# Two of the 32 output stores of a linear-attention kernel, cut by partitions into six transfers each

## The chip, the cores and the metric

The kernel runs on one core of a Trainium2 chip. A core has five engines with instruction streams of their own: TensorE (PE in the profile), VectorE (DVE), ScalarE (ACT), GpSimd (POOL) and SyncE (SP). It also has 16 DMA engines, which move data between the chip's main memory (HBM) and the on-chip memory (SBUF, 128 partitions). Here SP issues every transfer but one. The metric is the device time of one execution in microseconds (us); smaller is better. The time before is 171.07 us, the median of three runs (171.04 to 171.13).

## The reference

The inputs `q`, `k`, `v` are bf16, of one batch, 32 heads, 2048 rows and 128 columns. Every head is computed by itself:

```python
phi_q = where(q > 0, q + 1, exp(q)) + 1e-6
phi_k = where(k > 0, k + 1, exp(k)) + 1e-6
kv  = einsum("bhsd,bhse->bhde", phi_k, v)
z   = einsum("bhsd->bhd", phi_k)
num = einsum("bhqd,bhde->bhqe", phi_q, kv)
den = einsum("bhqd,bhd->bhq", phi_q, z)[..., None] + 1e-6
out = num / den
```

An input or an output of one head is 2048 x 128 bf16 values, 512 KB. The kernel reads three such blocks for each head and writes one: 50.33 MB in, 16.78 MB out.

## The kernel before

One head is one step of the pipeline. Its 2048 rows are laid out so that partition `p` holds the 16 rows `16p` to `16p + 15` (`rows`, L228): in SBUF and in HBM alike a partition's share is one contiguous run of 4096 bytes. A transfer of one head is therefore 128 runs of 4096 bytes (for `v`, 256 runs of 2048 bytes, because the tile in SBUF has a gap in the middle).

For each head (`for h in range(NH)`, L264) the kernel loads k, v and q (L281), forms the two parts of phi_k on ACT, POOL and DVE (L289 to L300), multiplies them with v on PE (L316, L319), transposes q on PE (L335), forms phi_q on ACT and DVE (L346 to L355), multiplies it with kv on PE (L370, L371), and divides by the denominator on DVE (L391, L397, L415, L419). In the last three heads a part of the division runs on ACT (L406, table `TAIL`). The result of a head lies in one of ten output buffers, `o_sb[:, bo]` with `bo = h % 10`, and goes to HBM by the store of L431.

The order of every engine's stream is written out by hand. `Plan.add` takes an engine, a key, what the operation reads and writes, and for a transfer the semaphore that it raises. `Plan.order` (L54) sorts each engine's operations by key, and `Plan.emit` (L60) puts the necessary waits ahead of each. A wait stops all that stands behind it in the same stream. At its end SP waits until the semaphore of every store has its full count (L118 to L121).

On SP, the loads of head `h` have keys `h - 7.95` (k), `h - 6.9` (q) and `h - 6.8` (v), and the store of head `h` has the key of this line:

```python
            late = h + 1.0 + 0.18 * h
```

So the stores fall further and further behind their heads. The last loads, those of head 31, have keys up to 24.2. The store of head 20 has the key 24.6, so the stores of heads 20 to 31 are all issued after the last load, in order of heads: ten whole ones, then head 30 in two pieces and head 31 in three (table `PIECES`, L181). Heads 22 and 25 are among the whole ones. Their buffers, 2 and 5, are not written again by any later head.

Of the kernel before, what the change touches and what calls it, by code (L numbers as in the profile page):

```python
# [144 lines left out]
def bass_standalone__linear_attn_elu__prompt_kernel(  # L145
# [8 lines left out]
    NT = 16  # L154
# [3 lines left out]
    NBI = 6  # L158
    NBO = 10
# [20 lines left out]

    PIECES = {NH - 2: ((0, 6), (6, NT)), NH - 1: ((0, 6), (6, 12), (12, NT))}  # L181
    EXTRA = {NH - 2: 0, NH - 1: 1}

    qf = q.rearrange("b h s d -> (b h) s d")
    kf = k.rearrange("b h s d -> (b h) s d")
    vf = v.rearrange("b h s d -> (b h) s d")
    of = out.rearrange("b h s d -> (b h) s d")

    with ExitStack() as es:
        def sb(name, shape, dt):  # L190
            return es.enter_context(nc.sbuf_tensor(name, shape, dt))
# [14 lines left out]
        o_sb = sb("o_sb", [P, NBO, NT, D], bf16)  # L206
# [11 lines left out]
        def dma_sem(name):  # L218
            return dsems[name]

        for n, c in (("k", NBI), ("q", NBI), ("v", NBI), ("o", NBO + 3), ("x", 2)):
            for i in range(c):
                dsems[(n, i)] = es.enter_context(nc.semaphore(f"s_{n}{i}"))

        block = es.enter_context(nc.Block())
        pl = Plan()

        def rows(x, h):  # L228
            return x[h].rearrange("(p j) d -> p (j d)", j=NT)
# [7 lines left out]
               reads=[("id0",)], writes=[("ident",)])  # L237
# [26 lines left out]
        for h in range(NH):  # L264
# [3 lines left out]
            bi, b2, b3, bo = h % NBI, h % 2, h % 3, h % NBO  # L268

            def load(name, buf, src, key, h=h, bi=bi):  # L270
# [7 lines left out]
                if name == "v":  # L278
# [11 lines left out]
                   reads=[("k", bi)], writes=[("ek", b2)])  # L290
            pl.add("pool", h, lambda g, bi=bi, b3=b3: g.tensor_scalar(rk_sb[:, b3, :], k_sb[:, bi, :], BIG, 0.0,  # L291
                                                                      op0=ALU.min, op1=ALU.max),
                   reads=[("k", bi)] + ([("emq", 1)] if h == 2 else []), writes=[("rk", b3), ("rkx", b3), ("phik", b3)])
            pl.add("dve", at("emk", -3 + 0.95),
                   lambda d, b2=b2, b3=b3: d.tensor_scalar(emk_sb[:, b3, :], ek_sb[:, b2, :], 1.0, EPS, op0=ALU.min, op1=ALU.add),  # L295
                   reads=[("ek", b2)], writes=[("emk", b3)])

            def added(x, b3=b3):
# [3 lines left out]
                reads=[("emk", b3), ("rkx", b3)] + ([("emq", (h - 1) % 3)] if h else []), writes=[("phik", b3)])  # L302

            def kv(pe, tiles, srcs, h=h, bi=bi, b3=b3):
                for j in tiles:
# [17 lines left out]
                   reads=[("emk", b3), ("rk", b3), ("v", bi), ("ones",), ("vones",)], writes=[("bankkv",)])  # L323
            pl.add("pe", at("kv", -1.2), lambda pe, kv=kv: kv(pe, ADD, (rk_sb,)), reads=[("phik", b3), ("v", bi)], writes=[("bankkv",)])
            pl.add("act", at("kvs", -0.95), lambda a, b3=b3: a.activation(kvs_sb[:, b3, 1:], kvz_ps[:, 1:NC], ACT.Copy),
                   reads=[("bankkv",)], writes=[("kvs", b3)])
            pl.add("dve", at("zs", -1 + 0.905), lambda d, b3=b3: d.tensor_scalar(  # L327
                kvs_sb[:, b3, 0:1], kvz_ps[:, 0:1], kvz_ps[:, NC:NC + 1], None, op0=ALU.add),
                   reads=[("bankkv",)], writes=[("zs", b3)])
# [14 lines left out]
            for half in (0, 1):  # L344
                pl.add("act", h - 1.1 + 0.05 * half,
                       lambda a, b2=b2, c=cols(half): a.activation(eq_sb[:, b2, c], xT_ps[:, c], ACT.Exp),  # L346
                       reads=[("bankx", half)], writes=[("eq", b2, half)])
            pl.add("act", h - 1.0,
                   lambda a, b3=b3, c=cols(1): a.activation(rq_sb[:, b3, c], xT_ps[:, c], ACT.Relu),  # L349
                   reads=[("bankx", 1)], writes=[("rq", b3, 1)])  # L350
            pl.add("dve", at("rq", -2 + 0.948),
                   lambda d, b3=b3, c=cols(0): d.tensor_scalar(rq_sb[:, b3, c], xT_ps[:, c], 0.0, None, op0=ALU.max),  # L352
                   reads=[("bankx", 0)], writes=[("rq", b3, 0)])
            pl.add("dve", at("emq", -2 + 0.955),
                   lambda d, b2=b2, b3=b3: d.tensor_scalar(emq_sb[:, b3, :], eq_sb[:, b2, :], 1.0, EPS, op0=ALU.min, op1=ALU.add),  # L355
                   reads=[("eq", b2, 0), ("eq", b2, 1)], writes=[("emq", b3)])
# [4 lines left out]
            def nbank(b, h=h):  # L361
                return ("bankx", b) if h == NH - 1 and b < 2 else ("banko", b)
# [48 lines left out]
            for g, (b0, b1, place_d, runs) in enumerate(groups):  # L411
# [6 lines left out]
                    reads=banks, writes=[("den", b3, g)])  # L418
                pl.add("dve", key + 0.01, lambda d, b3=b3, b0=b0, b1=b1: d.reciprocal(  # L419
                    rden_sb[:, b3, 4 * b0:4 * b1], den_sb[:, b3, 4 * b0:4 * b1]),  # L420
                    reads=[("den", b3, g)], writes=[("rden", b3, g)])
                if g == 0:
                    pl.add("dve", h + 0.911, last_tile, reads=[nbank(0), nbank(1), ("rden", b3, 0)], writes=[("o", bo, NT - 1)])
                for n, (eng, t0, t1, *place_a) in enumerate(runs):
                    pl.add(eng, h + place_a[0] if eng == "act" else key + 0.012 + 0.004 * n,
                           div_act(t0, t1) if eng == "act" else div(t0, t1),
                           reads=[nbank(b) for b in range(t0 // 3, (t1 + 2) // 3)] + [("rden", b3, g)],
                           writes=[("o", bo, t) for t in range(t0, t1)])

            def store(t0, t1, key, slot, h=h, bo=bo):  # L430
                pl.add("sp", key, lambda sp: sp.dma_start(rows(of, h)[:, t0 * D:t1 * D],  # L431
                                                          o_sb[:, bo, t0:t1].rearrange("p j d -> p (j d)")),
                       reads=[("o", bo, t) for t in range(t0, t1)], dma=("o", slot))

            late = h + 1.0 + 0.18 * h
            for n, (t0, t1) in enumerate(PIECES.get(h, ((0, NT),))):
                store(t0, t1, late + 0.01 * n, bo if n == 0 else NBO + EXTRA[h] + n - 1)

# [29 lines left out]
```

## Time and profile before

| What | Value |
|---|---|
| Median of three runs | 171.07 us |
| The profiled execution's own time | 171.07 us |
| Its span, from the first to the last instruction | 169.3 us |
| Granted TensorE clock, mean | 0.967 |
| Busy: PE, ACT, DVE, POOL | 159.0, 157.3, 149.7, 106.1 us |
| Moved by DMA | 67.56 MB, mean 399 GB/s |
| Stores issued by SP | 35: 30 of 512 KB, five smaller |

The time of the execution is 1.8 us longer than its span; that part lies outside what the profile shows. A busy share is the part of the span in which an engine had an instruction in work. The DMA share is the mean over the core's 16 DMA engines; because neighbouring packets of one engine overlap a little in the record, an engine that never pauses shows slightly more than 1.

### The profile page before, as it was taken

The page shows a single profiled execution, that of the slowest core. Times are in us where ns is not written, and L with a number is a line of the kernel's source. Part 1 is how long each engine was busy: PE and PEld are TensorE (multiplying, and loading weights), DVE is VectorE, ACT ScalarE, POOL GpSimd, SP SyncE. Part 2 cuts the span into 40 slices and gives each one's busy share as a digit, 9 for nine tenths or more (in the row PEclk, how much of TensorE's full clock was granted, in tenths as well). Part 3 has the DMA queues.
Part 4 walks back from the last instruction along what each step waited for, and adds up shares of the span by engine and source line. Part 5 has one row for each costly group of instructions (what it writes and reads, how often), then busy time and mean ns, then how long its engine had stood idle before and what let it go on. Part 6 is the DMA issues. An engine that isn't in the chain of part 4 may idle for free.

```text
span 169.3 us, 7126 instructions
## 1 busy us (share of the span) xinstructions
PE 159.0 (94%) x3116; PEld 158.0 (93%) x3116; DVE 149.7 (88%) x293; ACT 157.3 (93%) x179; POOL 106.1 (63%) x72
## 2 busy tenths in 40 slices
PE   7499999999999999999999999999999999999940
PEld 7399999999999999999999999999999999999830
DVE  0253899999999999999999999999999999999870
ACT  3789999999999999999999999999999999996960
POOL 2586866666677766666677766666667776666000
PEclk9957999999999999999999999999999999999995
DMA  5999999999999999999999999999999999999985
GB/s 190 415 416 408 416 408 406 406 406 415 409 411 409 413 413 411 414 412 411 418 410 411 417 407 412 413 414 411 413 413 411 411 415 413 409 416 415 401 348 195
DMA packets 22862, 67.56 MB, mean 399 GB/s; under 512 B 2096, under 2 KB 2608, under 8 KB 22832
## 3 DMA queue, kind: packets, MB, share of 16 engines
q1 hardware_dynamic: 22688, 66.59, 98.6%
q8 instruction: 24, 0.39, 0.9%
q10 hardware_dynamic: 144, 0.52, 0.8%
q14 instruction: 6, 0.05, 0.1%
HBM read 50.33 MB, written 16.78 MB: 396 GB/s over the span
## 4 chain that ended last, share of the span: by engine, by line
PE 90%; DMA 3%; DVE 3%; ACT 1%; issue 0%
PE kvz_ps L316 38%; PE o_ps L370 17%; PE x_ps L335 17%; PE o_ps L371 17%; DMA k_sb<-in_k_dram 3%; DVE o_sb L397 1%; PE kvz_ps L319 1%; ACT ek_sb L289 1%; DVE emk_sb L295 0%; DVE rden_sb L419 0%; DVE den_sb L415 0%; DVE o_sb L391 0%; DVE kvs_sb L327 0%
## 5 line engine op out<-in xcount | busy, mean ns | idle before, releaser
L300 POOL TENSOR_TENSOR rk_sb<-rk_sb,emk_sb 128x640 bf16<-128x640 bf16 x32 | 44.8, 1399 | 45.1 <-DVE emq_sb L355 41.3
L289 ACT ACTIVATE ek_sb<-k_sb 128x2048 bf16<-128x2048 bf16 x32 | 69.4, 2169 | 3.0 <-DMA k_sb<-in_k_dram 3.0
L346 ACT ACTIVATE eq_sb<-x_ps 128x1024 bf16<-128x1024 bf16 x64 | 69.5, 1258 | 2.2 <-PE x_ps L335 2.2
L316 PE MATMUL kvz_ps<-v_sb,rk_sb 128*128 128x128 bf16 (+1 forms) x512 | 69.0, 220 | 0.0
L397 DVE TENSOR_TENSOR o_sb<-o_ps,rden_sb 128x768 bf16<-128x768 f32 (+2 forms) x63 | 68.0, 1119 | 0.1
L291 POOL TENSOR_SCALAR rk_sb<-k_sb 128x2048 bf16<-128x2048 bf16 x32 | 61.1, 1909 | 5.0 <-DMA k_sb<-in_k_dram 3.4
L370 PE MATMUL o_ps<-kvs_sb,emq_sb 128*128 128x129 bf16 (+1 forms) x536 | 61.1, 217 | 0.3 <-DVE o_sb L397 0.3
L371 PE MATMUL o_ps<-kvs_sb,rq_sb 128*128 128x129 bf16 (+1 forms) x536 | 61.1, 217 | 0.0
L316 PE MATMUL kvz_ps<-v_sb,emk_sb 128*128 128x128 bf16 (+1 forms) x352 | 56.5, 221 | 1.5 <-DVE emk_sb L295 1.5
L319 PE MATMUL kvz_ps<-ones_sb,rk_sb 128*128 128x1 bf16 x388 | 53.9, 167 | 0.0
L370 PEld LDWEIGHTS o_ps<-kvs_sb,emq_sb 128*128 128x128 bf16 x536 | 50.6, 98 | 0.5 <-DVE o_sb L397 0.4
L371 PEld LDWEIGHTS o_ps<-kvs_sb,rq_sb 128*128 128x128 bf16 x536 | 50.1, 97 | 0.0
L316 PEld LDWEIGHTS kvz_ps<-v_sb,rk_sb 128*128 128x128 bf16 x512 | 47.8, 99 | 0.0
L349 ACT ACTIVATE rq_sb<-x_ps 128x1024 bf16<-128x1024 bf16 x32 | 40.6, 1270 | 0.0
L319 PE MATMUL kvz_ps<-ones_sb,emk_sb 128*128 128x1 bf16 x228 | 38.1, 168 | 0.0
L316 PEld LDWEIGHTS kvz_ps<-v_sb,emk_sb 128*128 128x128 bf16 x352 | 34.3, 99 | 1.6 <-issue 1.6
L335 PE MATMUL x_ps<-ident,q_sb 128*128 128x128 bf16 x512 | 34.7, 222 | 0.9 <-DMA q_sb<-in_q_dram 0.9
L319 PEld LDWEIGHTS kvz_ps<-ones_sb,rk_sb 128*128 128x128 bf16 x388 | 35.6, 96 | 0.0
L335 PEld LDWEIGHTS x_ps<-ident,q_sb 128*128 128x128 bf16 x512 | 30.7, 99 | 1.2 <-DMA q_sb<-in_q_dram 1.1
L295 DVE TENSOR_SCALAR emk_sb<-ek_sb 128x2048 bf16<-128x2048 bf16 x32 | 21.8, 683 | 10.2 <-ACT ek_sb L289 10.2
L352 DVE TENSOR_SCALAR rq_sb<-x_ps 128x1024 bf16<-128x1024 bf16 x32 | 21.8, 680 | 1.4 <-ACT eq_sb L346 1.4
L355 DVE TENSOR_SCALAR emq_sb<-eq_sb 128x2048 bf16<-128x2048 bf16 x32 | 22.2, 693 | 0.4 <-ACT eq_sb L346 0.4
(27 smaller groups left out, 89.8 us busy)
## 6 DMA issues: line engine op xcount, KB each, us to landing
k_sb<-in_k_dram SPq DMA_DIRECT2D x32, 512.0 KB, 13.0
v_sb<-in_v_dram SPq DMA_DIRECT2D x32, 512.0 KB, 13.5
q_sb<-in_q_dram SPq DMA_DIRECT2D x31, 512.0 KB, 13.1
out_dram<-o_sb SPq DMA_DIRECT2D x30, 512.0 KB, 13.6
out_dram<-o_sb SPq DMA_DIRECT2D x3, 192.0 KB, 4.6
q_sb<-in_q_dram ACTq DMA_DIRECT2D x1, 512.0 KB, 4.9
out_dram<-o_sb SPq DMA_DIRECT2D x1, 320.0 KB, 5.5
out_dram<-o_sb SPq DMA_DIRECT2D x1, 128.0 KB, 3.9
```

The costliest lines, as they stand in the source:

```text
L289: lambda a, bi=bi, b2=b2: a.activation(ek_sb[:, b2, :], k_sb[:, bi, :], ACT.Exp),
L291: pl.add("pool", h, lambda g, bi=bi, b3=b3: g.tensor_scalar(rk_sb[:, b3, :], k_sb[:, bi, :], BIG, 0.0, op0=ALU.min, op1=ALU.max), reads=[( ...
L300: pl.add("pool", h + 0.5, lambda g, added=added: g.tensor_tensor(out=added(rk_sb), in0=added(rk_sb), in1=added(emk_sb), op=ALU.add), reads ...
L316: last = pe.matmul(kvz_ps[:, 1 - l:NC + r], lhsT=w, rhs=rhs, start=first, stop=fin, skip_group_check=True)
L319: last = pe.matmul(kvz_ps[:, z:z + 1], lhsT=w, rhs=ones_sb[:, 0:1], start=False, stop=fin, skip_group_check=True)
L335: last = pe.transpose(xT_ps[:, j * P:(j + 1) * P], q_sb[:, bi, j * P:(j + 1) * P], ident[:])
L346: lambda a, b2=b2, c=cols(half): a.activation(eq_sb[:, b2, c], xT_ps[:, c], ACT.Exp),
L349: lambda a, b3=b3, c=cols(1): a.activation(rq_sb[:, b3, c], xT_ps[:, c], ACT.Relu),
L355: lambda d, b2=b2, b3=b3: d.tensor_scalar(emq_sb[:, b3, :], eq_sb[:, b2, :], 1.0, EPS, op0=ALU.min, op1=ALU.add),
L370: pe.matmul(o_ap, lhsT=emq_sb[:, b3, t * P:(t + 1) * P], rhs=kvs_sb[:, b3, c0:c1], start=True, stop=False)
L371: return pe.matmul(o_ap, lhsT=rq_sb[:, b3, t * P:(t + 1) * P], rhs=kvs_sb[:, b3, c0:c1], start=False, stop=True)
L397: return lambda d: d.tensor_tensor(out=o_sb[:, bo, t0:t1, :].rearrange("p (a b) d -> p a b d", b=n), in0=_ap(nfull(b), 512 * b + NC * (t0 ...
```

## The change

The stores of heads 22 and 25 are no longer one transfer of 128 partitions each. Each becomes six transfers, of 1, 2, 4, 8, 9 and 104 partitions, one behind the other in SP's stream at the place of the old store. Together they move the same bytes from the same buffer to the same place. Each of the twelve has a semaphore of its own, so SP's final wait covers 25 semaphores of stores instead of 13 (those of buffers 2 and 5 stay, for heads 2 and 12 and for 5 and 15). The streams of PE, DVE, ACT and POOL hold the same instructions in the same order as before; SP's has ten transfers more.

```diff
+    ROWS = (22, 25)
...
-        for n, c in (("k", NBI), ("q", NBI), ("v", NBI), ("o", NBO + 3), ("x", 2)):
+        for n, c in (("k", NBI), ("q", NBI), ("v", NBI), ("o", NBO + 15), ("x", 2)):
...
             late = h + 1.0 + 0.18 * h
+            if h in ROWS:
+                r0 = 0
+                for n, r in enumerate((1, 2, 4, 8, 9, 104)):
+                    pl.add("sp", late + 0.01 * n, lambda sp, h=h, bo=bo, r0=r0, r=r: sp.dma_start(
+                        rows(of, h)[r0:r0 + r, :], o_sb[r0:r0 + r, bo].rearrange("p j d -> p (j d)")),
+                        reads=[("o", bo, t) for t in range(NT)], dma=("o", NBO + 3 + 6 * ROWS.index(h) + n))
+                    r0 += r
+                continue
             for n, (t0, t1) in enumerate(PIECES.get(h, ((0, NT),))):
```

## The prediction

> **What bounds the kernel now.** I read the page first (span, slices, DMA queues, chain), then tables by stretches of time, then SP's own waits.
>
> ```profile
> span 169.3 us, 7126 instructions
> ...
> DMA  5999999999999999999999999999999999999985
> ...
> DMA packets 22862, 67.56 MB, mean 399 GB/s; under 512 B 2096, under 2 KB 2608, under 8 KB 22832
> ## 3 DMA queue, kind: packets, MB, share of 16 engines
> q1 hardware_dynamic: 22688, 66.59, 98.6%
> ...
> PE 90%; DMA 3%; DVE 3%; ACT 1%; issue 0%
> ```
>
> The chain of waits says PE, 90%. But in its order of time it ends with the last division on DVE (163.53 us, 0.96 us long): it says nothing of the 4.8 us from there to the end. The DMA engines are full in all slices but the first and the last, and SP's queue alone takes 98.6% of 16 engines' span. So the kernel has two walls of nearly the same height, and the end is set by the second. 131 transfers were issued (section 6 of the page: 32 + 32 + 31 + 30 + 3 + 1 + 1 + 1), and 2096 packets are under 512 B, exactly 16 for each: each of these 128-partition transfers has 16 completions, one for each engine, so each engine carries 8 of the 128 rows of 4096 bytes.
>
> Next the stretches (columns: length, busy time of PE, PEld, DVE, ACT, POOL, granted clock, DMA share, GB/s):
>
> ```profile
> 137.00:141.00 4.00, 4.00 (x87) 4.00 (x84) 3.99 (x6) 4.00 (x6) 2.83 (x2) 1.00 1.04 416
> 141.00:145.00 4.00, 4.00 (x88) 4.00 (x84) 3.97 (x9) 4.00 (x6) 3.26 (x2) 1.00 1.03 411
> 145.00:149.00 4.00, 4.00 (x85) 4.00 (x83) 3.97 (x9) 4.00 (x4) 2.96 (x2) 1.00 1.03 408
> 149.00:153.00 4.00, 4.00 (x84) 4.00 (x82) 3.96 (x9) 4.00 (x6) 2.53 (x3) 1.00 1.04 419
> 153.00:157.00 4.00, 4.00 (x84) 4.00 (x81) 3.96 (x9) 2.38 (x5) 2.42 (x2) 1.00 1.02 411
> ```
>
> ```profile
> 165.00:166.00 1.00, 0.00 (x0) 0.00 (x0) 0.00 (x0) 0.00 (x0) 0.00 (x0) 0.50 0.86 327
> 166.00:166.50 0.50, 0.00 (x0) 0.00 (x0) 0.00 (x0) 0.00 (x0) 0.00 (x0) 0.50 0.82 311
> 166.50:167.00 0.50, 0.00 (x0) 0.00 (x0) 0.00 (x0) 0.00 (x0) 0.00 (x0) 0.50 0.57 219
> 167.00:167.50 0.50, 0.00 (x0) 0.00 (x0) 0.00 (x0) 0.00 (x0) 0.00 (x0) 0.50 0.61 225
> 167.50:168.00 0.50, 0.00 (x0) 0.00 (x0) 0.00 (x0) 0.00 (x0) 0.00 (x0) 0.50 0.51 182
> 168.00:168.50 0.50, 0.00 (x0) 0.00 (x0) 0.00 (x0) 0.00 (x0) 0.00 (x0) 0.50 0.22 77
> ```
>
> The reader is to see two things. A fully used set of engines shows 1.03 and 413 GB/s (mean of the first five rows). And after 166.5 us, with nothing left to compute, the share stands at 0.57 and 0.61: 0.57 / 1.03 x 16 is 8.9 engines. So seven engines are through, and about nine still work off a backlog until 168.5 us. The last store was issued at 164.9 us and took 3.9 us to land; the early seven had moved their part of it 2 us sooner. The end of this kernel is the backlog of the nine **late** engines. A packet more on a late engine moves the end; a packet more on an early engine does not.
>
> SP's own waits from 150 us on:
>
> ```profile
> SPq L112 <- ACT o_sb L406: 8.1, 4, 5.4
> SPq L431 <- DVE o_sb L397: 4.0, 2, 3.2
> SPq L121 <- DMA out_dram<-o_sb: 3.2, 4, 1.2
> ```
>
> **The change part by part.**
>
> *Price of a row.* 413 GB/s over 16 engines is 25.8 GB/s; 4096 bytes take 0.159 us on one engine.
>
> *Where the rows go.* A whole store is 8 rows on each engine. The five small transfers hold 24 rows, and none can reach more engines than it has rows. No transfer of the trace has fewer than 128 rows, so the dealing is bounded. At one end, transfers start at different engines or follow the partitions, and each engine has 8 rows again: 0 us. At the other end, each transfer starts at the same engine and gives equal shares, as all 131 of the trace do. Then the first engine gets a row of each small transfer; 104 has no equal shares over 16, its widest equal split is 13 engines of 8 rows. In the order of dealing the 16 engines then get 13, 12, 11, 11, 10, 10, 10, 10, 9, 8, 8, 8, 8, 0, 0, 0 rows (sum 128). If 104 were split evenly (6.5 rows), the first would have 11 or 12. I take the second end: equal shares on 16 completions are what every row shows. For both stores the additions are +10, +8, +6, +6, +4 (four engines), +2 rows, none for four, and 16 fewer for three.
>
> [...]
>
> *What reaches the end.* If the first engine is late, the end moves by 10 x 0.159 = 1.59 us less the time by which that engine was done ahead of the last of the nine. From 167.5 us the nine did (0.51 + 0.22) x 0.5 x 16 / 1.03 = 5.7 engine-us, 0.63 us each of the 1.0 us until 168.5: a mean lead of 0.37 us, between 0 and about 0.8. So +1.2 us, with ends 0.8 and 1.6. If it is early, it has room: from 160 to 166.5 us the share is 0.93, 0.86, 0.88, 0.92, 0.82, 0.86, 0.82, which leaves 16 engine-us idle, 2.3 us for each of seven.
>
> *Ten more issues on SP.* A store's issue took 0.33 to 3.57 us, median 1.1 (line L431): 3.3 to 36 us, by the median 11 us. All twelve stand behind the last load, so no load waits for them. Behind them stand the stores of heads 23 to 31. SP's waits there are for results (3.2 and 5.4 us the longest, 8.6 us together), which absorb most; should the store of head 29 (issued at 159.4 us) go out 2.5 us late, it took 6.8 us to land where the very last took 3.9, so 2.9 us of it was queueing. Cost 0; it shows only if SP falls over 3 us behind. [...]
>
> *Ten more completions.* On the first engine at most 10 packets of 4 bytes: 0 us to (as if each were a row) 1.6 us. I take 0, as 8 rows and a completion together take 8 x 0.159 = 1.27 us per transfer at the measured rate.
>
> *Six more waits at SP's end.* 28 ns each (line L121), with the waits for the last pieces still behind them: covered by the 3.2 us that SP spends there; 0.2 us without that cover.
>
> *Buffers and the other engines.* Buffers 2 and 5 are not reused, and the other four streams are unchanged: 0, hidden or not.
>
> *Sum.* The profiled execution took 171.07 us, equal to the median: 169.3 of span and 1.8 around it, which stay. 171.07 + 1.59 - 0.37 = 172.3 us.
>
> **The rivals.**
>
> *R1: the first engine is early, a later one in the dealing is late.* The end moves by 1.27 - 0.37 = 0.9 us (second engine, 172.0), 0.6 (third or fourth, 171.65) or 0.25 (fifth to eighth, 171.3). For it: the trace names no engine numbers. The nine cannot all lie among the seven engines to which nothing is added, so at least two of them get rows.
>
> *R2: no change.* The rows are spread evenly after all, or the late engines that get rows are those with 0.6 us of lead: 171.07, at most 171.3. For it: nothing shows the dealing of small transfers. Against it: a one-row transfer can't be spread.
>
> *R3: faster.* The three engines relieved by 16 rows (2.5 us) are the last of the nine. Then the next late engine sets the end; the nine thin out between 167.5 and 168.5 us, so three of nine taken from the back give some 0.2 us at most: 170.85. It decides only if no late engine with less than 0.3 us of lead gets a row. Against it: six of the nine are not relieved.
>
> *R4: more than I count.* Equal shares could mean 8 engines of 13 rows for the 104 (10 extra rows for each store, 3.2 us, 173.9), or a small transfer could cost an engine more than its bytes (up to 1.6 us, 173.9).
>
> [...]
>
> **How the numbers follow.** Equal dealing from one engine: 0.86. Within it the first engine is late with 9/16, so 0.48 for the forecast; first early and second late 7/16 x 9/15 = 0.26, so 0.22; third or fourth 0.16, so 0.13; the rest of the 0.86 is about 0.02 and hidden. Even spread 0.07, faster 0.05, R4 0.03. This measurement can tell about 0.2%, 0.34 us, from no change. Slower by more: 0.48 + 0.22 + 0.12 + 0.03 = 0.85; faster by more: 0.04; within: 0.11. The range leaves out R2, R3 and R4: 171.3 to 172.7 (171.07 + 1.6 at the top); forecast 172.3, its own range 171.8 to 172.7.
>
> **What would show it.** The streams of compute end as before (last division near 164.5 us). After 166.5 us the DMA share falls further, to a few engines and at the very end one (0.06), and moving ends near 169.7 us; the span is near 170.5. The page counts 141 transfers and 2256 packets under 512 B if small transfers still make 16 completions; fewer show directly on how many engines they ran. The last store takes 5 us instead of 3.9 to land. I am wrong if the share keeps its shape (R2), if the tail becomes shorter (R3), or if the store of head 29 is issued well after 159.4 us (SP).

## The result, and the profile after

The changed kernel takes 171.79 us in the median (171.70 to 172.29), beside 171.10 us (171.04 to 171.29) for the kernel before on the same chip. The medians differ by 0.69 us. The ratio, which is taken over all executions and not from the two medians, is 1.0048 with a 95% interval of 1.0036 to 1.0060, that is 0.62 to 1.03 us: slower. The span was 169.9 to 170.0 us in all four executions. The profiled execution took 171.8 us, 170.0 of it the span, so the part outside the span is 1.8 us as before.

From the page of the changed kernel (span, DMA in 40 slices, packets, SP's queue, the chain by engine, and the rows of the stores by size):

```profile
span 170.0 us, 7142 instructions
...
DMA  5999999999999999999999999999999999999984
...
DMA packets 22904, 67.56 MB, mean 397 GB/s; under 512 B 2138, under 2 KB 2650, under 8 KB 22874
...
q1 hardware_dynamic: 22730, 66.59, 98.3%
...
PE 90%; DMA 3%; DVE 3%; ACT 1%; issue 0%
...
out_dram<-o_sb SPq DMA_DIRECT2D x28, 512.0 KB, 13.5
out_dram<-o_sb SPq DMA_DIRECT2D x2, 416.0 KB
```

The chain by engine has not changed at all, which shows how little it says of the end of this kernel. The number that tells most is the 2138 packets under 512 B. Before there were 2096, 16 completions for each of 131 transfers. Two whole stores took away 32 of them and the twelve new transfers brought 74, and 74 is 2 x (1 + 2 + 4 + 8 + 9 + 13). So 1 + 2 + 4 + 8 + 9 + 13 engines took part for each store: a transfer of r partitions up to nine ran on r engines, and the one of 104 on 13. The number of completions of each of the twelve transfers says the same.

The same stretches as shown of before (length, busy time of PE, PEld, DVE, ACT, POOL, granted clock, DMA share, GB/s):

```profile
149.00:153.00 4.00, 4.00 (x84) 4.00 (x82) 3.97 (x9) 4.00 (x6) 2.53 (x3) 1.00 1.04 417
153.00:157.00 4.00, 4.00 (x83) 4.00 (x81) 3.97 (x10) 2.32 (x5) 2.39 (x2) 1.00 1.02 409
...
166.00:166.50 0.50, 0.00 (x0) 0.00 (x0) 0.00 (x0) 0.00 (x0) 0.00 (x0) 0.50 0.87 330
166.50:167.00 0.50, 0.00 (x0) 0.00 (x0) 0.00 (x0) 0.00 (x0) 0.00 (x0) 0.50 0.54 209
167.00:167.50 0.50, 0.00 (x0) 0.00 (x0) 0.00 (x0) 0.00 (x0) 0.00 (x0) 0.50 0.87 323
167.50:168.00 0.50, 0.00 (x0) 0.00 (x0) 0.00 (x0) 0.00 (x0) 0.00 (x0) 0.50 0.45 164
168.00:168.50 0.50, 0.00 (x0) 0.00 (x0) 0.00 (x0) 0.00 (x0) 0.00 (x0) 0.50 0.30 107
168.50:169.00 0.50, 0.00 (x0) 0.00 (x0) 0.00 (x0) 0.00 (x0) 0.00 (x0) 0.50 0.13 46
169.00:169.50 0.50, 0.00 (x0) 0.00 (x0) 0.00 (x0) 0.00 (x0) 0.00 (x0) 0.50 0.01 4
```

Until 157 us nothing has moved: the same rate, and the same work on the compute engines. The last division on DVE starts at 163.49 us, before at 163.53. The difference is the tail. Before, the moving was over at 168.5 us with a last step of 0.22. Now about two engines (0.13 x 16 / 1.03 = 2.0) go on until 169.

The time at which each engine's completion of the very last store is stamped says it engine by engine, without naming the engines:

```
last store, completions of its 16 engines (us from the span's start)
before  166.58 166.59 166.60 166.61 166.64 166.68 166.75
        168.03 168.19 168.26 168.27 168.61 168.62 168.68 168.79 168.81
after   167.72 167.73 167.75 167.78 167.80 167.81 167.82 167.85 167.89
        168.42 168.48 168.57 168.59 168.92 169.36 169.53
```

The last engine is done 0.72 us later. The kernel is 0.69 us longer and the span 0.7. A completion follows the end of the moving by some tenths of a microsecond (the last packet ends at 168.47 us before and at 169.10 after, the last completion is stamped at 168.81 and at 169.53), so these times lie a little behind those of the stretches.

The change itself names some of the engines. The transfers of 1, 2, 4, 8 and 9 partitions of head 22 ran on as many engines, issued within 1.5 us of each other (145.0 to 146.3 us), so a stamp that is new against the smaller transfer belongs to an engine further on in the dealing. (Each of the twelve has one stamp more, right behind its issue, at 145.44 us for the first, which was issued at 144.97; it is left out here.)

```
partitions, and the completions of head 22's small transfers in the changed kernel
1   151.62
2   151.81 152.24
4   151.99 152.14 152.42 153.53
8   151.76 152.18 152.33 152.64 153.75 155.65 155.89 156.05
9   151.78 151.98 152.37 152.52 152.86 153.99 155.87 156.10 156.26
```

The first engine is early: 151.62 us. The first three are within some 0.4 us of each other, the fourth is 1.1 us behind the third. The step to eight partitions adds three stamps 4 us later, at 155.65 to 156.05, and one early one; the ninth is early again. (Which of the four is the early one is shown by an experiment below: the eighth.) So the fifth, sixth and seventh engine are the late ones here, and they are given 10 rows instead of 8 in each of the two stores.

SP's waits from 150 us on:

```profile
SPq L112 <- ACT o_sb L407: 7.7, 4, 5.4
SPq L121 <- DMA out_dram<-o_sb: 2.4, 4, 1.0
SPq L432 <- DVE o_sb L398: 2.0, 2, 1.6
```

SP still waits for results, so the ten issues did not make it the bound. The store of head 29 is issued at 159.38 us, before at 159.41. The last four issues take longer than before (0.68 to 1.16 us instead of 0.33 to 0.43), and the very last store goes out at 165.36 us instead of 164.90.

### The profile page after: what moved, and what is told of

It reads as the page before. It is cut to its first block, busy times and chain, and to the rows that moved or that the text cites. A ratio compares the mean times of both kernels' runs of the same rounds, so it can differ in the third digit from the quotient of the medians.

```text
span 170.0 us, 7142 instructions
## 1 busy us (share of the span) xinstructions
PE 159.0 (94%) x3116; PEld 157.9 (93%) x3116; DVE 149.8 (88%) x293; ACT 157.3 (93%) x179; POOL 106.1 (62%) x72
## 2 busy tenths in 40 slices
DMA packets 22904, 67.56 MB, mean 397 GB/s; under 512 B 2138, under 2 KB 2650, under 8 KB 22874
## 4 chain that ended last, share of the span: by engine, by line
PE 90%; DMA 3%; DVE 3%; ACT 1%; issue 0%
PE kvz_ps L317 38%; PE o_ps L371 17%; PE x_ps L336 17%; PE o_ps L372 17%; DMA k_sb<-in_k_dram 3%; DVE o_sb L398 1%; PE kvz_ps L320 1%; ACT ek_sb L290 1%; DVE emk_sb L296 0%; DVE rden_sb L420 0%; DVE den_sb L416 0%; DVE o_sb L392 0%; DVE kvs_sb L328 0%
## 5 line engine op out<-in xcount | busy, mean ns | idle before, releaser
L290 ACT ACTIVATE ek_sb<-k_sb 128x2048 bf16<-128x2048 bf16 x32 | 68.3, 2135 | 2.9 <-DMA k_sb<-in_k_dram 2.9
L347 ACT ACTIVATE eq_sb<-x_ps 128x1024 bf16<-128x1024 bf16 x64 | 68.4, 1223 | 2.3 <-PE x_ps L336 2.3
L350 ACT ACTIVATE rq_sb<-x_ps 128x1024 bf16<-128x1024 bf16 x32 | 39.6, 1237 | 0.0
```

What stands on the lines that cost most here:

```text
L290: lambda a, bi=bi, b2=b2: a.activation(ek_sb[:, b2, :], k_sb[:, bi, :], ACT.Exp),
```

## The experiments

Each kernel is the kernel before with the store of head 22, or those of heads 22 and 25, cut in another way. `SIZES` gives the numbers of partitions of the pieces in their order; the loop that issues them is that of the change, one semaphore for each piece. Differences are to the kernel before on the same chip in the same session, whose median was 171.05, 170.96 and 171.06 us for the three groups.

The theory to be tested (**rows**): a transfer runs on the largest number of engines, up to 16, that divides its partitions (as 128 did on 16, and in the change 1, 2, 4, 8, 9 and 104 on 1, 2, 4, 8, 9 and 13), always from the first engine on, in equal shares; the end moves by 0.159 us for each row that the late engines get more or fewer. Its rivals: the end moves with the **number** of transfers, completions or issues; or the pieces collide in some way that the count of rows does not hold.

### Which engines are late

One store in transfers of 1, 2, 3 and so on up to 15 partitions, so that each names one engine more.

```diff
+    SIZES = {22: (1, 2, 3, 4, 5, 6, 7, 8, 9, 10, 11, 12, 13, 14, 15, 8)}
```

> The store of head 22 alone in 16 transfers, of 1, 2, 3 and so on up to 15 partitions, and one of 8. If a transfer of n partitions (n up to 16) takes the n first engines with a row each, each transfer has one completion stamp more than the one ahead, and the new stamp names the next engine: this gives the lag of all but the last engine by its place in the dealing. Theory: the late ones are among engines five to eight and ten to sixteen. In time: engines five to eight get 4, 3, 2, 1 rows more, so the end moves by 0.15 to 0.65 us: 171.3 to 171.7 us. Rival, number of transfers: fifteen extra, 172.1 us.

One execution took 171.79 us, just above what the theory of rows had given (171.3 to 171.7). The completions of the transfers of 7 to 12 partitions; the new stamp of each step is told by comparison with the one before it:

```
7    152.76 152.77 153.16 154.39 155.86 156.13 156.31
8    151.49 152.95 152.95 153.34 154.58 156.06 156.37 156.57
9    151.63 151.69 153.13 153.13 153.52 154.76 156.26 156.58 156.78
10   151.80 151.90 153.31 153.31 153.70 154.94 155.86 156.47 156.79 156.99
11   151.98 152.11 153.48 153.50 153.88 154.50 155.12 156.03 156.66 156.99 157.19
12   152.16 152.32 153.67 153.68 154.07 154.69 155.31 156.21 156.39 156.88 157.20 157.41
```

The first, second, third, eighth and ninth engine are early, the fourth and the eleventh lie between, the fifth to seventh, the tenth and the twelfth are late. From 13 on the steps added only late stamps, so the 13th to 15th are late too; no step adds the 16th alone. The store of head 23 in the kernel before agrees: six completions are early (153.88 to 154.59 us), two lie between (155.61 and 156.76) and eight are late (158.01 to 158.71), so three of the last four engines are late. That fixes what each cut should do to the late ones.

### Rows taken from late engines, or added

Three cuts of head 22's store alone: 4 rows instead of 8 for the 4th to 14th engine and none for the last two, 19 instead of 8 for the first six, and 12 instead of 8 for the first ten.

```diff
+    SIZES = {22: (69, 56, 3)}
```

> The store of head 22 alone, in three transfers of 69, 56 and 3 partitions. 69 is shared by 3 engines (23 rows each), 56 by 14 (4 each), 3 by 3: the first three engines get 28 rows instead of 8, the next eleven 4, the last two none. By the probe the first three engines are early and have room. Theory of rows: the late engines have 4 rows (0.63 us) less, the three 20 rows (3.2 us) more, after which they end at about the same time: 170.4 us, faster by 0.6. If the three don't have that room: slower than 170.4. Rival, cuts cost by their number: 171.2 us. Rival, unequal transfers cost as such: over 172 us.

```diff
+    SIZES = {22: (102, 26)}
```

> The store of head 22 alone, in two transfers of 102 and 26 partitions. 102 is shared by 6 engines (17 rows each), 26 by 13 (2 each): the first six engines get 19 rows instead of 8, seven get 2, three none. By the probe engines five and six are late. Theory of rows: 11 rows more on them, 1.75 us, less a lead of up to 0.4: 172.4 to 172.8 us, with one extra transfer. This is the mirror of the run with 69, 56 and 3 partitions, which loads only early engines. Rival, cuts cost by their number: 171.1 us.

```diff
+    SIZES = {22: (40, 88)}
```

> The store of head 22 alone, in two transfers of 40 and 88 partitions. 40 is shared by 10 engines (4 rows each), 88 by 11 (8 each): ten engines get 12 rows instead of 8, one 8, five none. The first ten hold four late ones. Theory of rows: four rows more on late engines, as in the run with 24 and 104 partitions, 0.64 us: 171.7 us. That run cost 1.4 us; if a rise of four rows costs 1.4 us here too (172.4 us), the price of a row on a late engine is twice what its bytes say; if not, the rest of that run came from elsewhere.

The fourth is half the change, the six sizes for head 22 alone: 10 rows instead of 8 for the fifth to seventh engine.

```diff
+    SIZES = {22: (1, 2, 4, 8, 9, 104)}
```

> Only head 22's store in the six sizes (1, 2, 4, 8, 9, 104); head 25's stays whole. Rows on the late engines: engines five to seven in the dealing get 2 rows more (10 instead of 8) instead of 4. Row theory (the end moves by 0.16 us for each row on these engines): half of what the change itself cost, +0.35 us: 171.3 to 171.4. Rival, that the pieces themselves cost (number of transfers, fewer rows than 16 in one): with 5 more transfers instead of 10 the same half, so this run alone does not tell them apart; with a cost that comes only when both stores are cut it would be 171.0.

| Kernel | Transfers more | Rows more on the latest engines | x 0.159 us | Measured difference | Median; ratio with its interval |
|---|---|---|---|---|---|
| 69, 56, 3 | 2 | -4 | -0.64 | -0.55 | 170.41; 0.9970 (0.9961 to 0.9979) |
| head 22 alone, six sizes | 5 | +2 | +0.32 | +0.31 | 171.37; 1.0016 (1.0007 to 1.0025) |
| the change | 10 | +4 | +0.64 | +0.69 | 171.79; 1.0048 (1.0036 to 1.0060) |
| 40, 88 | 1 | +4 | +0.64 | +0.71 | 171.67; 1.0037 (1.0023 to 1.0052) |
| 102, 26 | 1 | +11 | +1.75 | +1.78 | 172.74; 1.0102 (1.0089 to 1.0115) |

All four new cuts fell where the row theory put them, within 0.1 us, and their pieces had the completions that it asks for: 3, 14 and 3; 6 and 13; 10 and 11; 1, 2, 4, 8, 9 and 13. The number of transfers has no such order: one transfer more costs 1.78 us or 0.71, ten cost 0.69, and two make the kernel faster.

The traces also say when the time arises. The store of head 26 is the first whole one behind head 25's place in SP's stream. Its last completion is already shifted by as much as the last completion of all:

| Kernel (one execution each) | Head 26, last completion | Difference | Very last completion | Difference |
|---|---|---|---|---|
| before | 162.44 us | | 168.81 us | |
| 69, 56, 3 | 161.91 us | -0.53 | 168.27 us | -0.54 |
| head 22 alone, six sizes | 162.63 us | +0.19 | 169.03 us | +0.22 |
| the change | 163.11 us | +0.67 | 169.53 us | +0.72 |
| 40, 88 | 163.00 us | +0.56 | 169.39 us | +0.58 |
| 102, 26 | 164.09 us | +1.65 | 170.39 us | +1.58 |

So the longer last issues and the additional waits of SP, which all stand behind that store in SP's stream, are not what costs the time.

The kernel with 69, 56 and 3 partitions is faster than both the kernel before and the change. Its tail (stretches as above):

```profile
166.50:167.00 0.50, 0.00 (x0) 0.00 (x0) 0.00 (x0) 0.00 (x0) 0.00 (x0) 1.00 0.75 276
167.00:167.50 0.50, 0.00 (x0) 0.00 (x0) 0.00 (x0) 0.00 (x0) 0.00 (x0) 0.61 0.56 199
167.50:168.00 0.50, 0.00 (x0) 0.00 (x0) 0.00 (x0) 0.00 (x0) 0.00 (x0) 0.50 0.14 48
```

The rows went to the first three engines, 28 instead of 8. Before, about nine engines worked from 166.5 us on and stopped at 168.5; here almost twelve (0.75 x 16 / 1.03) do, and all is over at 168. The same bytes end sooner because more engines share the end.

### Even pieces

If only the rows of an engine count, pieces that give every engine its 8 rows cost nothing. Two first tests, and one that takes 2 rows a store from the late engines by many small pieces:

```diff
+    SIZES = {22: (16, 16, 16, 16, 16, 48), 25: (16, 16, 16, 16, 16, 48)}
```

> Both stores in six transfers again, but of 16, 16, 16, 16, 16 and 48 partitions, so that each can be shared equally by 16 engines: 8 rows per engine and store as before. Theory of rows (the end moves only by rows added to engines that are late): 171.1 us, within 0.1 of the kernel before. Rival, number of transfers (each of the ten extra transfers costs some 0.07 us by its issue or completion): 171.8 us, as the changed kernel.

```diff
+    SIZES = {22: (64, 64), 25: (64, 64)}
```

> Both stores in two transfers of 64 partitions: four rows on each of 16 engines from each, so 8 rows per engine and store as before, with two extra transfers. Theory of rows: 171.05 us, within 0.1 of the kernel before. Rival, that a cut as such costs (six even transfers gave +0.7 us with ten extra ones): 0.07 each, 171.2 us.

```diff
+    SIZES = {22: (4, 4, 4, 4, 4, 4, 4, 4, 96), 25: (4, 4, 4, 4, 4, 4, 4, 4, 96)}
```

> Both stores in nine transfers: eight of 4 partitions (one row on each of four engines) and one of 96 (six rows on each of 16). The first four engines get 14 rows instead of 8, all others 6. Theory of rows: the completion stamps of the changed kernel say that the first four engines are not among the late ones, so every late engine loses four rows in the two stores, 0.63 us, and the four take 12 more, 1.9 us; one of the four is about 2.4 us behind and may become the last, so 170.5 to 170.7 us, faster. Rival, number of transfers: sixteen extra, 172.2 us. A rival that small transfers are costly in themselves: slower too.

All three missed the row theory. Pieces of 16: 171.76 us (171.16 to 172.86), ratio 1.0047 (1.0029 to 1.0064), which is what the rival, the number of transfers, had given. Halves: 173.02 us (172.26 to 174.29), 1.0123 (1.0092 to 1.0153), the slowest kernel of all, with only two transfers more, so that the number of transfers does not explain these kernels either. Pieces of 4: 171.16 us (170.59 to 172.02), 1.0002 (0.9987 to 1.0017), where only the fastest executions reached what the rows say. All three spread by 1.4 to 2 us from one execution to the next; the kernel before spreads by half a microsecond.

A further cut, of two transfers with 24 and 104 partitions, came out with the sign that the row theory gives and over twice its size: 172.46 us (172.28 to 172.56), ratio 1.0081 (1.0068 to 1.0094). That is 1.41 us, of which the rows (+4 on late engines) explain 0.64. The run with 40 and 88 partitions puts the same four rows on late engines and cost 0.71, so the other 0.77 us are not the price of a row.

```diff
+    SIZES = {22: (24, 104), 25: (24, 104)}
```

> Both stores in two transfers, of 24 and 104 partitions. 24 is shared by 12 engines (2 rows each), 104 by 13 (8 rows each): the first twelve engines get 10 rows instead of 8, four more for both stores, which is what engines five to eight get in the changed kernel. Theory of rows: four rows more on late engines, 0.64 us, so 171.7 to 171.8 us, with two extra transfers instead of ten. Rival, number of transfers: 2 x 0.07, 171.25 us.

The traces show two things in these kernels that the kernel before has not, or hardly. The first is SP in the kernel with pieces of 16, here as stretches, behind the row of the kernel before that the second of them is to be compared with:

```profile
157.00:160.00 3.00, 3.00 (x63) 2.85 (x62) 2.58 (x9) 3.00 (x9) 0.00 (x0) 1.00 1.01 407
```

```profile
153.00:157.00 4.00, 4.00 (x83) 4.00 (x81) 3.97 (x10) 2.43 (x5) 2.37 (x2) 1.00 0.96 354
157.00:160.00 3.00, 3.00 (x64) 2.85 (x60) 2.58 (x9) 3.00 (x9) 0.00 (x0) 1.00 0.78 273
160.00:163.00 3.00, 2.37 (x38) 1.93 (x35) 2.67 (x8) 2.54 (x10) 0.00 (x0) 1.00 0.97 388
163.00:166.00 3.00, 0.00 (x0) 0.00 (x0) 1.36 (x3) 1.15 (x5) 0.00 (x0) 1.00 1.00 394
166.00:168.00 2.00, 0.00 (x0) 0.00 (x0) 0.00 (x0) 0.00 (x0) 0.00 (x0) 0.69 1.01 376
```

Between 150.6 and 158.4 us six issues in a row take 0.97 to 1.85 us each; before, the issues from 146 us on took 0.33 to 1.68, and the long ones came where nothing waited for them. The store of head 26 goes out at 158.4 us instead of 148.1, and the DMA engines run dry to 0.78 and 273 GB/s. From then to 167 us SP goes from one issue to the next with 0.1 us between them at most, and all 16 engines end together, at 168.74 to 169.06 us. In this execution the end is set by SP, and the row theory, which assumes that late engines never want for work, does not apply. It took 171.34 us, so what made others as long as 172.86 us was not traced.

The second is slow packets. The table has the packets of 4096 bytes that start between 156 and 162 us, when they belong to stores:

| Kernel | Packets | Mean | Over 250 ns | Longest | Time of the last four issues |
|---|---|---|---|---|---|
| before | 571 | 161 ns | 4 | 440 ns | 0.33 to 0.43 us |
| the change | 567 | 163 ns | 7 | 441 ns | 0.68 to 1.16 us |
| 24, 104 | 544 | 170 ns | 28 | 645 ns | 0.75 to 1.20 us |
| 64, 64 | 552 | 166 ns | 15 | 500 ns | 1.07 to 1.28 us |
| eight of 4, 96 | 548 | 172 ns | 20 | 926 ns | 1.08 to 1.19 us |
| five of 16, 48 | 448 | 178 ns | 29 | 1112 ns | 0.50 to 1.20 us |

That these packets account for the rest of the time in the four kernels below the change is not shown: a packet's engine is not in the trace.

### What about the halves costs

Three runs take the halves apart: one store in halves instead of two; two stores by even and odd partitions; and two stores by columns, each transfer with all 128 partitions and half of each row.

```diff
+    SIZES = {22: (64, 64)}
```

> Only head 22's store cut into two halves of 64 partitions; head 25's stays whole. Every engine has 4 + 4 rows as before. Row theory: 171.0, no change. If each cut into halves of the partitions has a price of its own (two cost 2.0 us together): about 172.0. If the price comes from two cut stores standing near each other in the queue: 171.0 to 171.3.

```diff
+    SIZES = {22: (64, 64), 25: (64, 64)}
...
-                        rows(of, h)[r0:r0 + r, :], o_sb[r0:r0 + r, bo].rearrange("p j d -> p (j d)")),
+                        rows(of, h)[r0::2, :], o_sb[r0::2, bo].rearrange("p j d -> p (j d)")),
```

> Heads 22 and 25 cut into two transfers of 64 partitions each, as in the run of the halves, but of the even and the odd partitions instead of the lower and the upper half. Number of transfers, rows and engines are those of the run of the halves (173.0). [...] If it is the number of rows per engine in a transfer (4 instead of 8) that costs: 173.0 again.

```diff
-                        rows(of, h)[r0:r0 + r, :], o_sb[r0:r0 + r, bo].rearrange("p j d -> p (j d)")),
+                        rows(of, h)[:, 16 * r0:16 * (r0 + r)], o_sb[:, bo].rearrange("p j d -> p (j d)")[:, 16 * r0:16 * (r0 + r)]),
```

> Heads 22 and 25 cut into two transfers each, along the columns: both take all 128 partitions, the first the first 2048 bytes of each, the second the rest. [...] If the half of the partitions costs: 171.0 to 171.3 (the loads of v are runs of 2048 bytes too and go at the full rate). If an additional transfer in the late queue costs in itself, 0.5 to 1 us for each: 172 to 173.

| Cut of heads 22 and 25 | Median | Ratio with its interval | Over 250 ns; longest | Last four issues |
|---|---|---|---|---|
| lower and upper half | 173.02 us | 1.0123 (1.0092 to 1.0153) | 15; 500 ns | 1.07 to 1.28 us |
| the same, head 22 alone | 171.16 us | 1.0011 (0.9995 to 1.0027) | 3; 441 ns | 0.51 to 0.72 us |
| even and odd partitions | 171.13 us | 1.0004 (0.9996 to 1.0013) | 4; 434 ns | 0.33 to 0.42 us |
| by columns | 171.14 us | 1.0004 (0.9995 to 1.0013) | 4; 441 ns | 0.33 to 0.42 us |

The tails of the two that differ in nothing but which partitions go together, the halves first and then the even and odd partitions:

```profile
167.00:167.50 0.50, 0.00 (x0) 0.00 (x0) 0.00 (x0) 0.00 (x0) 0.00 (x0) 0.50 0.84 312
167.50:168.00 0.50, 0.00 (x0) 0.00 (x0) 0.00 (x0) 0.00 (x0) 0.00 (x0) 0.50 0.63 228
168.00:168.50 0.50, 0.00 (x0) 0.00 (x0) 0.00 (x0) 0.00 (x0) 0.00 (x0) 0.50 0.23 83
168.50:169.00 0.50, 0.00 (x0) 0.00 (x0) 0.00 (x0) 0.00 (x0) 0.00 (x0) 0.50 0.10 37
169.00:169.50 0.50, 0.00 (x0) 0.00 (x0) 0.00 (x0) 0.00 (x0) 0.00 (x0) 0.50 0.07 24
```

```profile
167.00:167.50 0.50, 0.00 (x0) 0.00 (x0) 0.00 (x0) 0.00 (x0) 0.00 (x0) 0.50 0.59 219
167.50:168.00 0.50, 0.00 (x0) 0.00 (x0) 0.00 (x0) 0.00 (x0) 0.00 (x0) 0.50 0.60 216
168.00:168.50 0.50, 0.00 (x0) 0.00 (x0) 0.00 (x0) 0.00 (x0) 0.00 (x0) 0.50 0.20 68
168.50:169.00 0.50, 0.00 (x0) 0.00 (x0) 0.00 (x0) 0.00 (x0) 0.00 (x0) 0.50 0.01 2
```

The halves keep one engine (0.07 x 16 / 1.03 = 1.1) busy to 169.5 us; the interleaved cut has the tail of the kernel before. The traced execution of the halves was the fastest of its six, 172.26 us. In it a single engine falls behind while the pieces of head 25 move: the store of head 26 has its last completion at 163.66 us and the one before that at 162.75, where the interleaved cut has 162.53 and 162.40. To the end the halves gain no further lag on the kernel before (+1.22 us at head 26, +1.07 at the end), so their long last issues, which stand behind that store, do not cause it.

The two cuts have the same 133 transfers, the same 16 completions of each (2128 packets under 512 B in both) and, in equal shares, the same 4 rows on each engine in each of their pieces. So neither the additional transfer nor the smaller share per engine costs anything that shows (0.07 us, and the ratio's interval holds 1); what costs here is that the pieces of the two stores are blocks of neighbouring partitions. The slow packets go and come with the cost. The long issues do not quite: they are there in part with one store in halves (0.51 to 0.72 us). One store in halves costs nothing in the median, though two of its eleven executions took 172.10 and 172.23 us; two stores in halves cost in all six. A partition's row goes to its own place in HBM, so a block of partitions is also a block of addresses there; these runs do not tell the two sides apart.

## Why the prediction was right, and where it was not

The forecast was 172.3 us and slower; the result is 171.79 us and slower, inside the range of 171.3 to 172.7 and just under the forecast's own, 171.8 to 172.7. The structure held and one step failed: which engines are late, and how much room the late ones have. That the time came out so near the forecast is in part luck.

**What bounds the kernel now** held. The streams of compute ended where they did before, and the end moved with the rows of late engines in five kernels, downwards too. In four other kernels, with both stores cut into blocks, the rows alone did not give the time.

**Price of a row** held: 0.159 us a row gives -0.64, +0.32, +0.64, +0.64 and +1.75 us; measured were -0.55, +0.31, +0.69, +0.71 and +1.78. Four rows more cost 1.41 us with 24 and 104 partitions, where something beyond the rows came in.

**Where the rows go** held to the packet: the second end, with 104 partitions on 13 engines, gives the 2138 small packets that were counted. The probe shows that the smaller transfers all start at the same engine: each step from 7 to 12 partitions adds one completion to the pattern of the one before. Which number an engine has is not in the trace. R4's first half (104 on 8 engines) and R2's even spread are ruled out by the same number.

**What reaches the end** failed. The step assumed that the first engine is late, with a chance of 9/16, and charged its 10 rows. The first engine is early, and so are the second and the third; the fourth is in between. What came true is the last case of R1, the fifth to eighth engine late, which was given a chance of 0.02 and 171.3 us. Its price was wrong as well: 4 rows less a mean lead of 0.37 us makes 0.27 (0.25 in the prediction), and 0.69 was measured. A mean lead over nine engines may be subtracted for an engine picked at random among them. It may not for a group of three to which the same rows are added: the latest of the three counts, and here its lead was nearly nothing (0.64 us of rows against 0.69 measured). And the chances of the cases were multiplied as if lateness fell on the engines at random, while the early ones stand in groups in the dealing (first to third, eighth and ninth). Two errors of opposite sign, too many rows and too large a lead, made a forecast that is 0.5 us off look nearer than its mechanism was.

**Ten more issues on SP** was right in its value, 0, for this kernel. The small issues took 0.24 to 0.39 us, far less than the median of 1.1 us that would have been the worry. But the four last issues grew from 0.33 to 0.43 us to 0.68 to 1.16, which no step foresaw; the last store went out at 165.36 us instead of 164.90. It did not count because the late engines still had work. The traces bear this out: the lag of 0.7 us is there at head 26's store, which stands ahead of those four. In the kernel with pieces of 16 longer issues (six in a row of 0.97 to 1.85 us) did set the end of the traced execution, so the 0 holds for the change and not for every cut.

**Ten more completions**, **six more waits at SP's end** and **buffers and the other engines**: 0 held, or nearly. All together they have the room between 0.64 us of rows and the 0.69 measured (0.62 to 1.03 by the interval).

**R3** had its mechanism right and its reach wrong. The last three of the dealing were relieved, and at least two of them are late. But three more late engines got rows, so the relief could not reach the end. Relieving all late engines, as 69, 56 and 3 partitions do, is what it needed, and then it is worth 0.55 us and not 0.2.

**What would show it**: moving ends near 169.7 us was forecast, it ended soon after 169 (share 0.13 until then and 0.01 behind it), with the last completion at 169.53; a span of 170.5, measured 170.0; the last store to land after 5 us, measured 4.2, as it was issued 0.46 us later.

## What to carry to other kernels

The last stretch of this kernel is a backlog on some DMA engines, and the bytes on those engines set its time: four rows more on the late ones cost 0.69 and 0.71 us, four fewer gained 0.55 us. The number of partitions of a late transfer decided where its bytes went: 104 ran on 13 engines, 102 on 6, 69 on 3. In a kernel that may end in this way, work out for each piece on how many engines it runs before cutting a transfer, and find out which engines are late: one transfer each of 1, 2, 3 and more partitions showed it here in their completions. Where a cut is needed, try columns or interleaved partitions, which cost 0.08 and 0.07 us here; two stores cut into blocks of neighbouring partitions cost up to 2.06 us with every engine's share unchanged, and why is open.

## What the runs showed of the hardware that was not expected

- Two stores cut into lower and upper halves cost 2.06 us, the same cut into even and odd partitions 0.07 us (the ratio's interval holds 1).
- Which engines are late is nearly the same in the three traces that name them (the change, half the change, the probe) and does not follow from the transfers, which gave all 16 engines equal shares for 140 us (16 completions for each). The spread at head 22 was 4.3 us in the changed kernel (151.76 to 156.05 us at eight partitions). The page has a queue of instruction packets, 24 of 16 KB, and one takes 0.96 us on its engine in the median. On which engines they ran is not in the trace, and what makes the late engines late is not shown.
- Issuing one of the last four stores, all of 128 partitions, takes 0.33 to 0.43 us before and with the interleaved and the column cuts, and 0.5 to 1.3 us in nearly all of these issues in the kernels cut into blocks of partitions. They are long without slow packets too: 0.56 to 0.80 us with 69, 56 and 3 partitions, where 3 packets are over 250 ns beside 4 before. Their cause stays open.
